# Three pairs of an output projection in Strassen's form, with their stage reordered

## The chip, the cores and the metric

The kernel runs on one core of one Trainium2 chip. TensorE (PE) multiplies, VectorE (DVE), ScalarE (ACT) and GpSimd (POOL) do the elementwise work, and SyncE (SP) issues nearly all the DMAs. Each engine takes its own instructions strictly in order and waits for the others through semaphores. The metric is the device time of one execution in microseconds, as the median of several runs.

## The reference

The kernel computes a transformer layer for 2048 tokens of 1024 features: linear attention with 32 heads of 32 features, then a gated feed-forward network (FFN) with 3584 hidden features. All inputs and the output are bf16.

```python
h  = x + A(layernorm(x), wqkv, wo)
h2 = h + B(layernorm(h), W_gate, W_up, W_down)

# A: q, k, v = split(x @ wqkv); phi(t) = where(t > 0, t + 1, exp(t)) + 1e-6
kv  = einsum("bhsd,bhse->bhde", phi(k), v)
z   = einsum("bhsd->bhd", phi(k))
num = einsum("bhqd,bhde->bhqe", phi(q), kv)
den = einsum("bhqd,bhd->bhq", phi(q), z)[..., None] + 1e-6
A   = (num / den) @ wo

# B: (relu(x @ W_gate) * (x @ W_up)) @ W_down
```

The change concerns the last line of A, `(num / den) @ wo`, and the addition of x to it.

## The kernel before

**Planning.** The program is written as calls of `PL.add(engine, ...)` and its wrappers `mm` (a matmul), `ident_act` (a copy on ACT), `dma` and `dma_t` (a transfer, or one that transposes, issued by SP). The order of the calls is the order on each engine. A `_Buf` remembers who wrote and read a buffer, and from that the waits are derived; `.over` names the buffers that lived in the same place before. So the order of work is written out by hand, mainly by functions put into lists (`hooks`) that are called between the products of a group.

**Stages.** Tokens come in 16 tiles of 128. The projections to k, v and q are made in Strassen's form by `sgroup`: of a pair of blocks on either side, seven products instead of eight, on four PSUM banks a, f, b and c. ACT copies the bank of one product to the next bank (`fk1`, `fk2`), so that later products accumulate on it; sums of inputs are made ahead on DVE. The FFN is in that form too: `t_sums` makes sums of its first weights (tiles T), `s_sums` the four sums S1 to S4 of the normalised h, `x_inner` and `w_inner1` sums for a second level of the scheme, and `ffn_unit` computes two gate or up column blocks at a time.

**The stage between.** It starts when the last q group has ended and its left-over feature maps (`late_phi`, two pairs of instructions at L879 and L882, on DVE) remain. One loop runs `t` from 4 to 20, with a lag of `LAG = NOT = 4` steps between numerators and projection:

```python
for t in range(NE, NST + LAG + 1):
    if LAG <= t < NST + LAG:
        a4_mm(t - LAG)
    if t < NST:
        a2_num(t)
        a2_div(t)
    if LAG <= t < NST + LAG:
        a4_h(t - LAG)
        run(late_phi, 1)
    if LAG + 1 <= t < TPP + LAG + 1:
        a4_norm(t - LAG - 1)
```

- `a2_num` (L1253) makes the numerators and denominators of one tile on PE: 32 small matmuls into banks 0 to 3.
- `a2_div` (L1264) divides on DVE: `dtmp` (L1270), `rden` (L1273) and `o` (L1275); then SP transposes o into a slot of the ring oT (`T3d`, L591).
- `a4_mm` (L1286) multiplies oT of a tile with wo: 2 halves of 512 columns, 8 matmuls each, into banks 4 and 5 or 6 and 7 in turn.
- `a4_h` (L1295) adds x in one DVE instruction of 128x1024 (`h`, L1299), stores h, and for tiles 0 to 7 starts the layer norm's statistics: two passes on ACT (L835) and four tiny POOL instructions (L841 to L1315).
- `a4_norm` (L1321) normalises on ACT one step later; SP then transposes into hnT (`T5d`).
- `load_x2` fetches x for a tile; the first eight have places of their own, the others share three.

Some of the FFN's preparation is spread over the same loop: from t = 9 one of the eight POOL sums of `t_sums` (L1401) per step, at t = 15 to 18 the sums S (L1377), at t = 4, 5, 17 and 18 a weight load. Then the FFN begins: the products P1 of its first unit, which are copied on to banks 4 and 5 by ACT, then P5, P2, P5, P6 and `r15` (L1625), whose second part R5 reads what `x_inner` (L1444) and `w_inner1` (L1422) made on DVE.

Of the kernel before, what the change touches and what calls it, by code (L numbers as in the profile page):

```python
# [6 lines left out]
ALU = mybir.AluOpType  # L7
# [125 lines left out]
def bass_sequential_preLN__linear_attn_block__glu_gated_reglu__prompt_kernel(  # L133
# [71 lines left out]
    with es:  # L205
# [8 lines left out]
        NV = 6  # L214
        NXN = 4
        NO = 4
        NOT = 4
        NDT = 4
        NWG = 6
        NTR = 4  # L220
# [4 lines left out]
        NWR = 2  # L225
        NSTAT = 4
        NX2 = 3
        NHS = 3
        NPH = 4

# [42 lines left out]
            return pk[:, i, :] if i < NPK else x1[:, i - NPK, :]  # L273

        osb = RE[:, 0:NO * D].rearrange("p (a b) -> p a b", a=NO)
        oT = RE[:, NO * D:(NO + NOT) * D].rearrange("p (a g t) -> p a g t", a=NOT, g=NG)
        ftmp = RE[:, 0:(NO + NOT) * D].bitcast(f32).rearrange("p (a b) -> p a b", b=SBW)
        c22 = RE[:, 2 * D:3 * D].rearrange("p (a b) -> p a b", b=SBW)
        c12 = RE[:, 3 * D:4 * D].rearrange("p (a b) -> p a b", b=SBW)
        xs5 = RE[:, 4 * D:6 * D].bitcast(f16).rearrange("p (j k t) -> p j k t", j=4, k=2)  # L280
        g5 = RE[:, 6 * D:8 * D].bitcast(f16).rearrange("p (s j c) -> p s j c", s=2, j=4)
        hnE = RE[:, 4 * D:8 * D].rearrange("p (t a c) -> p t a c", t=STB, c=P)
        o0 = (NO + NOT) * D
        x2r = RE[:, o0:o0 + NX2 * D].rearrange("p (a b) -> p a b", a=NX2)
        x2e = RC[:].rearrange("p (a b) -> p a b", a=TPP)

        def x2_slot(st):
            return st if st < TPP else TPP + st % NX2

        def x2(st):  # L290
            return x2e[:, st, :] if st < TPP else x2r[:, st % NX2, :]

        hl = RE[:, o0:o0 + 2 * D].rearrange("p (a b) -> p a b", a=2)
        xl = RE[:, o0 + 2 * D:o0 + 4 * D].rearrange("p (a b) -> p a b", a=2)
# [33 lines left out]
        D1 = RXH[:].bitcast(f16).rearrange("p (q t) -> p q t", t=SBW)  # L328
        Et = RX[:, 0:NPH * NW].rearrange("p (a b) -> p a b", a=NPH)
        btmp = RX[:, NPH * NW:(NPH + 4) * NW].bitcast(f32).rearrange("p (a b) -> p a b", a=2)  # L330

        def TWq(j):
            if j < 2:
# [27 lines left out]
        def bank(b, w=512):  # L361
            return ps[:, b, 0:w]
# [7 lines left out]
        def slots(name, n):  # L370
            return [_Slot(sem("%s%d" % (name, i))) for i in range(n)]
# [3 lines left out]
        sl_wkv = [slots("dwkv%d_" % i, 2) for i in range(NKV)]  # L375
        sl_wq = slots("dwq_", ND2)
        sl_wo = slots("dwo_", ND2)
        sl_x2 = slots("dx2_", TPP + NX2)
        sl_w = slots("dw_", NWG)
        sl_wd = slots("dwd_", NWS + NWX)  # L380
        sl_hr = slots("dhr_", NHR)
# [18 lines left out]
        def bufs(name, n):  # L400
            return [_Buf("%s%d" % (name, i)) for i in range(n)]
# [22 lines left out]
        B_dt = bufs("dt_", NDT)  # L424
        B_rd = bufs("rd_", NDT)
        B_oT = bufs("oT_", NOT)
        B_x2 = bufs("x2_", TPP + NX2)
        B_hs = bufs("hs_", NHS)
        B_hscr = bufs("hscr_", NST)
        B_hl = bufs("hl_", 2)  # L430
# [54 lines left out]
        def flat(x):  # L485
            return [b for row in x for b in (flat(row) if isinstance(row, list) else [row])]
# [5 lines left out]
            for b_ in B_pk[NPK + i]:  # L492
                b_.over = B_x1[i]
        kv_ring = flat(B_x1) + flat(B_pk) + flat(B_v) + [B_vones]
        for b_ in B_o + B_oT + B_x2[TPP:]:
            b_.over = kv_ring
        for b_ in B_x2[0:TPP]:
            b_.over = B_TWk
        for b_ in B_f + B_c22 + B_c12:
            b_.over = B_o + B_oT  # L500
        for b_ in B_hl + B_xl:
            b_.over = B_x2[TPP:]
        for b_ in flat(B_T):
            b_.over = B_wq
        for b_ in B_S:
# [15 lines left out]
            b_.over = flat(B_Sx[0:3])  # L521
        for b_ in B_hnT:
            b_.over = B_Sx[3] + B_TWq[0:2]
        for b_ in B_D1:
            b_.over = B_xn + B_hs
        for b_ in flat(B_lsum):
            b_.over = B_E + B_bt + [B_TWq[2]]
        for b_ in B_hres + B_ds:
            b_.over = B_lsum
        for b_ in B_outst:  # L530
            b_.over = B_E + B_bt + [B_TWq[2]]
        B_m5r.over = flat(B_wsum)
        for b_ in flat(B_g1a) + [B_m5a]:
            b_.over = flat(B_xnT) + flat(B_pqT)
        for b_ in B_xs1a:
            b_.over = B_E + B_bt + [B_TWq[2]]
        for b_ in B_hnE:
            b_.over = B_o + B_oT
        for b_ in B_V:
            b_.over = B_hnE  # L540
        for b_ in flat(B_hh) + B_out2:
            b_.over = flat(B_xnT) + flat(B_pqT)
        for b_ in flat(B_pqT):
            b_.over = flat(B_wkv)
        B_TWq[3].over = [B_zeros]
# [44 lines left out]
        def dma_t(slot, dst_ap, src_ap, name, reads=(), writes=()):  # L590
            return PL.add("sp", lambda e: e.dma_start_transpose(dst_ap, src_ap), reads=reads, writes=writes,  # L591
                          slot=slot, name=name)
# [301 lines left out]
        def run(ops, n):  # L894
            for _ in range(min(n, len(ops))):
                ops.pop(0)()
# [367 lines left out]
        def a2_div(st):  # L1264
            k = st % NO
            kd = st % NDT
            kt = st % NOT
            rb = [B_bank[b_] for b_ in NB]
            nv = ps[:, 0:HPG, 0:NG * NUW].rearrange("p h (g w) -> p g h w", w=NUW)
            PL.add("dve", lambda e: e.tensor_scalar(  # L1270
                out=dtmp[:, kd, :].rearrange("p (g h) -> p g h", h=HPG), in0=nv[:, :, :, Dh],
                scalar1=1e-6, scalar2=None, op0=ALU.add), reads=rb, writes=[B_dt[kd]], name="dtmp_%d" % st)
            PL.add("dve", lambda e: e.reciprocal(out=rden[:, kd, :], in_=dtmp[:, kd, :]),  # L1273
                   reads=[B_dt[kd]], writes=[B_rd[kd]], name="rden_%d" % st)
            PL.add("dve", lambda e: e.tensor_tensor(  # L1275
                out=osb[:, k, :].rearrange("p (g h e) -> p g h e", h=HPG, e=Dh),
                in0=nv[:, :, :, 0:Dh],
                in1=rden[:, kd, :].rearrange("p (g h) -> p g h", h=HPG).unsqueeze(3).to_broadcast([P, NG, HPG, Dh]),
                op=ALU.mult), reads=rb + [B_rd[kd]], writes=[B_o[k]], name="o_%d" % st)
            dma_t(sl_to[kt], oT[:, kt, :, :], osb[:, k, :], "T3d_%d" % st, reads=[B_o[k]], writes=[B_oT[kt]])  # L1280

        H_PAIRS = [4, 6]

        a4_bank = {}

        def a4_mm(st):  # L1286
            k = st % NOT
            b = a4_bank[st] = min(H_PAIRS, key=lambda b: max(bank_last[b], bank_last[b + 1]))
            for nt in range(ND2):
                touch_bank(b + nt)  # L1290
                for ct in range(NG):
                    mm(bank(b + nt, NW), oT[:, k, ct, :], wo[:, ct, nt * NW:(nt + 1) * NW],
                       ct == 0, ct == NG - 1, [B_oT[k], B_wo[nt]], B_bank[b + nt], "a4_%d_%d" % (st, nt))

        def a4_h(st):  # L1295
            xs = x2_slot(st)
            hs = st % NHS
            b = a4_bank.pop(st)
            PL.add("dve", lambda e: e.tensor_tensor(out=hsb[:, hs, :], in0=ps[:, b:b + 2, :],  # L1299
                                                    in1=x2(st).rearrange("p (a c) -> p a c", a=2), op=ALU.add),  # L1300
                   reads=[B_bank[b], B_bank[b + 1], B_x2[xs]], writes=[B_hs[hs]], name="h_%d" % st)
            if TPP <= st and st + NX2 < NST:
                load_x2(st + NX2)
            dma(sl_hs[hs], ov[st * P:(st + 1) * P, :], hsb[:, hs, :], "st_h_%d" % st, reads=[B_hs[hs]],
                writes=[B_hscr[st]])
            if st >= TPP:
                return
            ks = st % 2
            a4_k[st] = ks
            src = hsb[:, hs, :]  # L1310
            for f_ in act_stats(src, [B_hs[hs]], xn[:, st % NXN, :], B_xn[st % NXN], s2[:, ks, 0:4], B_s2[ks],
                                "ln2_%d" % st):
                f_()
            m_, r_, n_ = s2[:, ks, 0:1], s2[:, ks, 2:3], s2[:, ks, 4:5]
            PL.add("pool", lambda e: e.tensor_scalar(out=n_, in0=m_, scalar1=r_, scalar2=-1.0, op0=ALU.mult,  # L1315
                                                     op1=ALU.mult),
                   reads=[B_s2[ks][0], B_s2[ks][2]], writes=[B_s2[ks][4]], name="lnn_%d" % st)
# [3 lines left out]
        def a4_norm(st):  # L1321
            hs = st % NHS
            ks = a4_k[st]
            kx = st % NXN
            PL.add("act", lambda e: e.activation(out=xn[:, kx, :], in_=hsb[:, hs, :], func=ACTF.Identity,
                                                 bias=s2[:, ks, 4:5], scale=s2[:, ks, 2:3]),
                   reads=[B_hs[hs], B_s2[ks][2], B_s2[ks][4]], writes=[B_xn[kx]], name="norm2_%d" % st)
            dma_t(sl_tx[kx], hnT[:, :, st * P:(st + 1) * P], xn[:, kx, :], "T5d_%d" % st, reads=[B_xn[kx]],
                  writes=[B_hnT[st]])

# [908 lines left out]
                    for i in range(TPP + NX2):  # L2239
                        load_x2(i)  # L2240
        flush()
        LAG = NOT
        pool_t = t_sums(0, "pool")
        for t in range(NE, NST + LAG + 1):
            if LAG <= t < NST + LAG:
                a4_mm(t - LAG)
            if t < NST:
                a2_num(t)
                a2_div(t)
            if LAG <= t < NST + LAG:  # L2250
                a4_h(t - LAG)
                run(late_phi, 1)
            if LAG + 1 <= t < TPP + LAG + 1:
                a4_norm(t - LAG - 1)
            if t in (4, 5, 17, 18):
                load_w_next()
            if t >= 9:
                run(pool_t, 1)
            if 15 <= t < 19:
                s_sums()[t - 15]()  # L2260
        for q in range(NWR):
            load_wraw(q)
        load_w_next()
# [179 lines left out]
```

## Time and profile before

| What | Value |
|---|---|
| Runs | 717.06, 717.28, 717.21 us; median 717.21 |
| Profiled execution | span 714.8 us from its first to its last instruction; its device time is not listed apart |
| Granted TensorE clock | 1.000 over the span |
| The stage, 165.82 to 226.08 us | 60.26 us; PE busy 60.26, DVE 48.12, ACT 29.19, POOL 19.50 |
| Its last part, 204.45 to 226.08 us | 21.63 us; DVE busy 16.80, ACT 0.67, POOL 6.00 |

Lines of the timeline give the start in microseconds from the span's start, the duration in microseconds, the engine, the line of the kernel, the operation, out<-in by name, the shape, and how many equal instructions were merged (x16). In square brackets stands the idle time of the engine before, and what ended it. Names such as RE, RX, RXH, RC, RAB and RWG are large areas of SBUF in which several buffers live; ps is PSUM. A line of the chain gives start, duration, and what the time went to. A line of the windows gives the stretch, its length, the busy time and number of instructions of PE, PEld (weight loads), DVE, ACT and POOL, the granted clock, the busy share of the DMA engines and their GB/s.

### The profile page before, as it was taken

Reading aid. Unit: us, or ns where it says so; the run is one execution under the profiler, and the core shown is the slowest. Engines: PE = TensorE matmul, PEld = TensorE weight load, DVE = VectorE, ACT = ScalarE, POOL = GpSimd, SP = SyncE. Lnnn points to the kernel's source line nnn. Section 1 sums busy time; section 2 is a strip of 40 time slices with the busy share of each in tenths; the row PEclk is TensorE's granted clock in tenths of the full one; section 3 lists DMA queues with packets and bytes.
Section 4 is the critical chain, followed back from the end, with each engine's and each line's share of the span. In section 5 each row is a group of like instructions: output and inputs, shape, how many; then the busy total and the mean of one; then the engine's idle time right before and its main releaser. Section 6 shows DMA issues by size and latency. Waiting matters only on the chain.

```text
span 714.8 us, 13206 instructions
## 1 busy us (share of the span) xinstructions
PE 709.6 (99%) x5051; PEld 394.6 (55%) x5051; DVE 603.0 (84%) x964; ACT 404.3 (57%) x729; POOL 109.5 (15%) x178
## 2 busy tenths in 40 slices
PE   9999999999999999999999999999999999999998
PEld 4444444444444445455544558865555555548887
DVE  6988867899777799999998787878889888988984
ACT  4987667764841677777776411037666767633010
POOL 3221100000360223132312001310000000000331
PEclk9999999999999999999999999999999999999999
DMA  9853344015999799999897999995344544268996
GB/s 296 263 103 76 42 136 164 1 31 98 229 185 296 224 326 276 313 290 293 265 302 209 296 253 319 320 214 161 96 135 113 145 121 122 75 206 262 321 313 181
DMA packets 195103, 144.20 MB, mean 202 GB/s; under 512 B 53984, under 2 KB 172512, under 8 KB 195040
## 3 DMA queue, kind: packets, MB, share of 16 engines
q1 hardware_dynamic: 190048, 138.77, 66.9%
q0 software_dynamic: 4032, 3.67, 3.6%
q10 hardware_dynamic: 960, 0.92, 0.4%
q8 instruction: 40, 0.66, 0.4%
q14 instruction: 23, 0.19, 0.1%
HBM read 98.76 MB, written 32.51 MB: 184 GB/s over the span
## 4 chain that ended last, share of the span: by engine, by line
PE 95%; DVE 3%; DMA 1%; issue 1%; ACT 1%
PE ps L795 94%; DMA RAB<-RXH 1%; DVE RC L1018 0%; DVE RW L1018 0%; DVE RWG L1043 0%; DMA RE<-in_A_x_dram 0%; ACT RXH L835 0%; PE ps L956 0%; DVE RE L1796 0%; DVE st L809 0%; DVE RX L1134 0%; PE ps L935 0%; DVE RWG L1736 0%; DVE RH L1043 0%; DVE RE L1195 0%
## 5 line engine op out<-in xcount | busy, mean ns | idle before, releaser
L800 ACT ACTIVATE ps<-ps 128x512 f32<-128x512 f32 (+1 forms) x257 | 129.6, 516 | 188.7 <-PE ps L795 145.3
L795 PE MATMUL ps<-RC,RO 128*128 128x512 f16 x616 | 147.0, 369 | 0.0
L795 PEld LDWEIGHTS ps<-RC,RO 128*128 128x128 f16 x616 | 60.1, 98 | 53.2 <-ACT ps L800 1.2
L800 ACT ACTIVATE RE<-ps 128x512 f32<-128x512 f32 (+3 forms) x106 | 63.8, 627 | 32.2 <-PE ps L795 18.1
L795 PE MATMUL ps<-RC,RWG 128*128 128x512 f16 x320 | 80.9, 379 | 0.0
L795 PE MATMUL ps<-RH,RWG 128*128 128x512 bf16 (+1 forms) x348 | 77.7, 348 | 0.0
L795 PE MATMUL ps<-RH,RO 128*128 128x512 bf16 (+1 forms) x256 | 65.3, 379 | 0.0
L1805 POOL DMA_DIRECT2D out_dram<-RX x20 | 17.9, 1259 | 271.4 <-DVE RX L1796 218.3
L1535 DVE TENSOR_TENSOR RE<-ps,RE 128x1024 bf16<-128x1024 f32 (+1 forms) x42 | 44.0, 1047 | 18.2 <-PE ps L795 18.1
L795 PE MATMUL ps<-RW,RE 128*128 128x512 bf16 x256 | 57.6, 380 | 0.0
L795 PEld LDWEIGHTS ps<-RH,RWG 128*128 128x128 bf16 x348 | 34.0, 98 | 35.2 <-ACT ps L800 0.2
L795 PE MATMUL ps<-RW,RAB 128*128 128x256 f16 (+3 forms) x362 | 52.9, 301 | 0.0
L795 PE MATMUL ps<-RAB 128*128 128x512 bf16 (+2 forms) x238 | 49.8, 348 | 0.0
L795 PEld LDWEIGHTS ps<-RC,RWG 128*128 128x128 bf16 (+1 forms) x320 | 30.0, 98 | 34.4 <-ACT ps L800 5.8
L795 PEld LDWEIGHTS ps<-RW,RAB 128*128 128x128 f16 (+1 forms) x362 | 35.3, 98 | 14.5
L1535 DVE TENSOR_TENSOR RAB<-ps,RE 128x1024 bf16<-128x1024 f32 x28 | 34.2, 1221 | 10.1 <-PE ps L795 9.7
L1796 DVE TENSOR_TENSOR RE<-ps,RE 128x512 f32<-128x512 f32 x44 | 30.2, 686 | 14.4 <-PE ps L795 11.8
L1547 ACT ACTIVATE RAB<-RAB 128x1024 bf16<-128x1024 bf16 x28 | 29.5, 1053 | 19.6 <-DVE RAB L1535 19.6
L1535 DVE TENSOR_TENSOR RAB<-RAB,RE 128x1024 bf16<-128x1024 bf16 x56 | 37.2, 685 | 2.9 <-ACT RE L800 2.5
L795 PEld LDWEIGHTS ps<-RW,RE 128*128 128x128 bf16 x256 | 24.0, 98 | 27.9 <-DVE RXH L1299 0.4
L1401 DVE TENSOR_TENSOR RO<-RWG 128x1024 f16<-128x1024 bf16 x54 | 39.4, 729 | 0.0
L1401 DVE TENSOR_TENSOR RO<-RWG,RO 128x1024 f16<-128x1024 bf16 x54 | 38.2, 708 | 0.0
(188 smaller groups left out, 1229.1 us busy)
## 6 DMA issues: line engine op xcount, KB each, us to landing
RWG<-in_B_W_gate_dram SPq DMA_DIRECT2D x28, 512.0 KB, 5.9
RWG<-in_B_W_up_dram SPq DMA_DIRECT2D x28, 512.0 KB, 5.0
RW<-l_scr SPq DMA_DIRECT2D x20, 448.0 KB, 5.2
RW<-in_B_W_down_dram SPq DMA_DIRECT2D x14, 512.0 KB, 6.3
t_scr<-RW SPq DMA_DIRECT2D x14, 512.0 KB, 4.5
l_scr<-RX SPq DMA_DIRECT2D x7, 1024.0 KB, 9.5
RE<-l_scr SPq DMA_DIRECT2D x15, 448.0 KB, 4.5
RE<-in_A_x_dram SPq DMA_DIRECT2D x23, 256.0 KB, 3.7
```

Of the source, the lines that this page charges most:

```text
L795: lambda e: e.matmul(out_ap, lhsT, rhs, start=start, stop=stop, skip_group_check=skip),
L800: PL.add("act", lambda e: e.activation(out=dst, in_=src, func=func), reads=reads, writes=writes, name=name)
L1401: PL.add(eng, lambda e: e.tensor_tensor(out=tb(j, u), in0=f0(u), in1=f1(u), op=ALU.subtract), reads=[B_w[i + x] for x in r] + ([B_T[k + x] ...
L1535: PL.add("dve", lambda e: e.tensor_tensor(out=dst, in0=in0, in1=in1, op=op), reads=reads, writes=writes, name=name)
L1547: PL.add("act", lambda e: e.activation(out=d, in_=d, func=ACTF.Relu), reads=[], writes=db, name=name)
L1796: PL.add(eng, lambda e: e.tensor_tensor(out=dst, in0=in0, in1=in1, op=op), reads=reads, writes=writes, name=name)
L1805: PL.add("pool", lambda e: e.dma_start(dst, src, accum_op=ALU.add), reads=[bsrc], writes=[B_hscr[st]], slot=sl, name="acc_%d_%d" % (st, dh))
```

## The change

Tiles 0 to 9 (`NDIR = 10`) are projected as before. Tiles 10 and 11, 12 and 13, 14 and 15 become three groups in Strassen's form (`o_group`), with seven products of four matmuls each.

- The sums of wo (`wo_sums`, tiles TWo) are made on POOL, in eight instructions of half a matrix each: two before the loop, six after the steps 0 to 5.
- The sums of oT (`o_sums`, So1 to So4 per pair) are made on DVE, but for one of the first pair on POOL.
- In the groups, POOL adds x to the two shared parts (`add_x`, named ox). In the first two groups (`act_first`), the two direct outputs go through an ACT copy and a POOL add, and in the last one they are read by DVE. The other two are finished by DVE from a bank and the shared part.
- Numerators move to places within the projections (`at`); they run ahead of their use by other distances, and oT gets six slots (two of them in the area RX). Transposes of the normalised tiles 4 to 7 are issued later (`a4_t`). x of the tiles 12 to 15 gets places of its own in the area RA, loaded during the groups. The POOL sums of `t_sums`, the sums S and two weight loads move later.

```diff
-        NOT = 4
+        NOT = 6
+        NDIR = 10
 
+            dma_t(sl_to[kt], oT(st), osb[:, k, :], "T3d_%d" % st, reads=[B_o[k]], writes=[B_oT[kt]])
...
+        def wo_sums(j, eng, k0, k1):
...
+            x, y = {2: lambda: (w(1, 1), w(0, 1)), 0: lambda: (w(0, 1), w(0, 0)), 1: lambda: (w(1, 1), t(0)),
+                    3: lambda: (w(1, 0), t(1))}[j]()
+            PL.add(eng, lambda e: e.tensor_tensor(out=t(j)[0], in0=x[0], in1=y[0], op=ALU.subtract),
+                   reads=x[1] + y[1], writes=[B_TWo[j]], name="TWo%d" % (j + 1))
...
+        def o_group(p, bks, hooks, act_first):
+            sa, sb2 = 2 * p, 2 * p + 1
+            a, f, b, c = bks
+            s7, sc = (btmp[:, 1, :], B_bt[1]), (btmp[:, 0, :], B_bt[0])
...
+            def add_x(src, st, h, dst=None):
+                x, bx = res(st, h)
+                d, db = src if dst is None else dst
+                PL.add("pool", lambda e: e.tensor_tensor(out=d, in0=src[0], in1=x, op=ALU.add),
+                       reads=[bx] + ([] if dst is None else [src[1]]), writes=[db], name="ox_%d_%d" % (st, h))
+
+            def fin(st, h, bk, s=None):
+                d, db = half(st, h)
+                if s is not None:
+                    PL.add("dve", lambda e: e.tensor_tensor(out=d, in0=bank(bk), in1=s[0], op=ALU.add),
+                           reads=[B_bank[bk], s[1]], writes=[db], name="h_%d_%d" % (st, h))
+                elif act_first:
+                    ident_act(Ef[:, h, :], bank(bk), [B_bank[bk]], [B_Ef[h]], "oc_%d_%d" % (st, h))
+                    add_x((Ef[:, h, :], B_Ef[h]), st, h, (d, db))
+                else:
+                    x, bx = res(st, h)
+                    PL.add("dve", lambda e: e.tensor_tensor(out=d, in0=bank(bk), in1=x, op=ALU.add),
+                           reads=[B_bank[bk], bx], writes=[db], name="h_%d_%d" % (st, h))
...
+            prod(a, X(0, 0), W(0, 0), True, "P1")
+            ident_act(bank(b), bank(a), [B_bank[a]], [B_bank[b]], "ofk1")
+            hook(1)
+            prod(f, SX(2), TW(2), True, "P7")
+            ident_act(s7[0], bank(f), [B_bank[f]], [s7[1]], "os7")
+            add_x(s7, sb2, 0)
+            hook(2)
+            prod(b, SX(1), TW(1), False, "P6")
+            ident_act(bank(c), bank(b), [B_bank[b]], [B_bank[c]], "ofk2")
+            hook(3)
+            prod(a, X(1, 0), W(1, 0), False, "P2")
+            fin(sa, 0, a)
+            hook(4)
+            prod(c, SX(0), TW(0), False, "P5")
+            ident_act(sc[0], bank(c), [B_bank[c]], [sc[1]], "osc")
+            add_x(sc, sb2, 1)
+            hook(5)
+            prod(b, X(1, 1), TW(3), False, "P4")
+            fin(sb2, 0, b, s7)
+            hook(6)
+            fin(sb2, 1, f, sc)
+            store(sb2)
+            prod(c, SX(3), W(1, 1), False, "P3")
+            o_pend[1] = [lambda: fin(sa, 1, c), lambda: store(sa)]
+            hook(7)
...
-        LAG = NOT
         pool_t = t_sums(0, "pool")
...
+        at = {0: {15: [nd]}, 1: {14: [nd]}, 2: {13: [nd]}, 3: {11: [nd]}, 4: {9: [nd]}, 5: {7: [nd]},
+              6: {5: [nd]}, 7: {3: [nd]}, 8: {2: [nd, t5(4)]}, 9: {2: [nd, t5(5)]}}
+        aft = {0: [tw(2, 0)], 1: [tw(2, 2)], 2: [tw(1, 0)], 3: [tw(1, 2)], 4: [tw(3, 0)], 5: [tw(3, 2)],
+               8: sums(p0, (2, "pool")), 9: sums(p0, (0, "dve"), (1, "dve"), (3, "dve"))}
+        tw(0, 0)()
+        tw(0, 2)()
+        for d in range(NDIR):
+            a4_mm(d, at.get(d, {}))
+            a4_h(d)
+            run(late_phi, 1)
+            if 1 <= d <= TPP:
+                a4_norm(d - 1)
+            if d < 2:
+                load_w_next()
+            for f_ in aft.get(d, ()):
+                f_()
+            if d in (6, 7, 8):
+                run(pool_t, 1)
+        o_group(p0, [4, 6, 5, 7], {
+            2: [nd], 4: sums(p0 + 1, (2, "dve"), (0, "dve")), 5: [nd, lambda: load_x2(13), lambda: load_x2(12)],
+            6: sums(p0 + 1, (1, "dve"), (3, "dve")) + [t5(6), t5(7)]}, True)
+        load_w_next()
+        o_group(p0 + 1, [4, 2, 5, 7], {
+            1: [lambda: run(pool_t, 1)], 2: sums(p0 + 2, (2, "dve"), (0, "dve"), (1, "dve"), (3, "dve")),
+            3: [lambda: run(pool_t, 1), lambda: load_x2(15), lambda: load_x2(14)], 6: [ss[0], ss[1]]}, True)
+        load_w_next()
+        run(pool_t, 1)
+        o_group(p0 + 2, [4, 6, 5, 7], {2: [ss[2]], 4: [ss[3]]}, False)
+        for f_ in o_pend.pop(1):
+            f_()
+        run(pool_t, len(pool_t))
```

`nd` is `a2_num` and `a2_div` of the next tile. `tw(j, k0)` is half a weight sum, `t5` a held-back transpose, `ss` the four sums S, and `p0` is 5, the first pair in the new form. In `at`, the number before a list is the matmul (0 to 15) of that tile before which its entries are placed.

## The prediction

> **What bounds the kernel now.** I read the page first (busy shares, slices), then the chain that ended last, then the windows of the stage that the change rewrites, and last its timeline, engine by engine.
>
> ```profile
> PE 709.6 (99%) x5051; PEld 394.6 (55%) x5051; DVE 603.0 (84%) x964; ACT 404.3 (57%) x729; POOL 109.5 (15%) x178
> 44.03 630.50 PE ps L795 x4452
> 165.82:226.08 60.26, 60.26 (x641) 27.25 (x640) 48.12 (x66) 29.19 (x43) 19.50 (x40) 1.00 0.92 208
> 188.69 0.37 PE L795 MATMUL ps<-kvz,RAB 32*128 32x33 bf16 x32
> 189.00 3.63 PE L795 MATMUL ps<-RW,RE 128*128 128x512 bf16 x16
> 192.56 0.37 PE L795 MATMUL ps<-kvz,RAB 32*128 32x33 bf16 x32
> ```
>
> The first line is the page's: TensorE busy for 99% of the span. The second is the chain's: from 44.03 us it is 630.5 us of matmuls and nothing else. The third is the stage's window (total, then PE, PEld, DVE, ACT, POOL, granted clock, DMA share, GB/s): TensorE covers all 60.26 us at clock 1.00, and VectorE is at 80% (48.12). The last three are one step: numerators at 188.69, 16 matmuls from 189.00, the next numerators at 192.56, so 3.87 us. Single matmuls of 512 columns start 0.2159 us apart in the trace; 16 are 3.45 us and the numerators take the other 0.41. Check: 256 x 0.2159 + 12 x 0.41 = 60.2 us, the window. There is no slack on TensorE: a matmul less is a gain, and a wait is a loss.
>
> **What is removed.** A pair of tiles takes 2 x 2 x 8 = 32 matmuls, in Strassen's form 7 x 4 = 28. Three pairs: 12 x 0.2159 = 2.59 us off the path. The twelve numerators remain. The forks (ACT copying one bank to the next between products) are those of the projection stages, whose matmuls after a fork start 0.238 and 0.249 us after the one before instead of 0.216; two a group make 6 x 0.03, call it +0.2 us. So with full cover: -2.4 us.
>
> **What is added, and where it lies.** Weight sums: 8 POOL instructions of 128x1024. The nearest rows are 128x512 (1.152 us) and 128x256 (0.668), so 0.184 + 1024 x 0.00189 = 2.12 us each. The first two run before the loop, the others one a step behind the statistics of layer norm. Per pair: four sums of 128x512 (DVE 0.42 us as in L1043, POOL 1.15) and four adds of x or, in the first two groups, two on the shared halves and two behind an ACT copy; so 4, 4 and 2 POOL adds of 128x512 f32 (1.15 us, from L1796's undisturbed ones). In exchange the six h of 1.21 us on DVE become 8 of 0.69. Five of the eight POOL sums of the first FFN weights (1.15 us, before at 196 to 210 us) and all of S1 to S4 (1.21 us each, DVE, before among plain tiles) now fall among or behind the groups. Count of POOL work from the second group on: 7 adds and 5 sums, 13.8 us, where the trace had 6.0 us in the last 21.6. Whether that is hidden depends on whether POOL and DVE can run at once:
>
> ```profile
> 257.76 1.22 POOL L774 TENSOR_TENSOR RAB<-RW 128x256 f16<-128x256 bf16 x1 [2.19 <-PE ps L795]
> 258.37 1.16 DVE L1401 TENSOR_TENSOR RO<-RWG,RO 128x1024 f16<-128x1024 bf16 x1
> 259.45 0.68 DVE L1401 TENSOR_TENSOR RO<-RWG 128x1024 f16<-128x1024 bf16 x1
> 673.00 3.04 POOL L1796 TENSOR_TENSOR RE<-RE,RX 128x512 f32<-128x512 f32 x2 [1.13 <-DVE RE L1796]
> 675.17 1.83 DVE L1736 TENSOR_TENSOR RWG<-RAB 128x1792 f16<-128x1792 bf16 x1
> 205.40 1.23 DVE L1275 TENSOR_TENSOR RE<-ps,rden 128x1024 bf16<-128x1024 f32 x1
> 205.96 2.26 POOL L1401 TENSOR_TENSOR RO<-RWG 128x512 f16<-128x512 bf16 x2
> ```
>
> At 257.76 a POOL instruction of 0.67 us takes 1.22 because a DVE sum with both inputs in SBUF is under way; the next DVE sum then takes 1.16 instead of 0.68: each waits for the other's whole instruction, in order of arrival. The same at 673 to 677 for just the POOL add that the groups use (two in 3.04; a DVE sum of 1.08 takes 1.83). DVE work that reads PSUM (205.40) runs at its usual 1.23 beside POOL. So sums on DVE (So, S, x_inner, g1) and everything on POOL must be laid end to end; evacuations need not. That decides two places.
>
> **Place one: numerators of tile 7.**
>
> ```profile
> 175.63 1.21 DVE L1299 TENSOR_TENSOR RXH<-ps,RC 128x1024 bf16<-128x1024 f32 x1
> 176.47 0.27 POOL L1315 TENSOR_SCALAR s<-s 128x1 f32<-128x1 f32 x1
> 176.76 0.28 DVE L879 TENSOR_SCALAR RX<-RX 128x512 bf16<-128x512 bf16 x1
> 177.08 0.69 DVE L882 SCALAR_TENSOR_TENSOR RAB<-RXH,RX 128x512 bf16<-128x512 f32 x1
> 178.52 1.23 DVE L1275 TENSOR_TENSOR RE<-ps,rden 128x1024 bf16<-128x1024 f32 x1
> ```
>
> After h of tile 1 DVE still has a late feature map (176.76, 177.08; both inputs in SBUF), then o of tile 6 (178.52 to 179.75). At 176.47 POOL ends the statistics of tile 0, and there, some 0.22 us later, the change queues a 2.12 us weight sum: 176.7 to 178.8. The feature map then waits, and dtmp, rden and o of tile 6 queue behind it: o ends 2.0 to 2.1 us later, near 181.8. Before, numerators 7 came at 180.97; now they stand before matmul 11 of tile 3, at 177.40 + 11 x 0.2159 = 179.78, and need o's banks. TensorE waits 2.0 us. Bounds: 0 (the two DVE forms are not seen blocked in the trace; only tensor-tensor sums are) and 2.1; I take 2.0 since L882 too reads twice from SBUF. [...] Later steps have only PSUM readers on DVE, and per step 1.33 us of statistics and 2.12 of sums fit POOL's 3.87.
>
> **Place two: from the second group into the FFN.** Time 0 is the start of the first group; a product is 0.863 us, numerators 14 and 15 lie inside, so the groups would begin at 0, 6.87, 12.9 and the FFN at 19.0. Numerators 15 start at 4.73; dtmp, rden and o end at 7.2; their transpose lands about 3.7 us later (the stage's 14 transposes: 3.5 median, 5.2 worst), at 10.9. SP issues x of tiles 13 and 12 only behind that transpose and its 1.24 us of issuing: they land at 12.2 and 12.7 (3.7 median). DVE stops at the four sums of the third pair until the transpose lands, and everything behind it waits: h of tile 13, S1, S2, h, S3, and on to the FFN. POOL, free at 9.25, has its adds and weight sums queued. Laid end to end in order of arrival: add 10.4, T 11.6, So3 12.0, (x of 13) So1 12.4, add 13.5, So2 14.0, T 15.1, So4 15.5, add 16.7 beside h of tile 13 (16.2), S1 17.9, add 19.1, S2 20.3, T 21.4, S3 22.6, add 23.8, S4 25.0, add 26.1, add 27.3, h of tiles 15 and 14 until 28.7, behind two more T (29.6), x_inner 31.2, g1 31.6. TensorE needs h of tile 13 by 14.2 (fork of the third group into that bank: first loss, 2.1 us) and x_inner and g1 at R5 of the first FFN unit, 19.0 + 6.05 + 0.2 = 25.2. It gets there at 31.6: +6.3 us in all, the first 2.1 within it. The bounds: without the mutual blocking the same queue gives h of 13 at 14.1, the last h at 22.8 and g1 at 24.9, just before 25.2, so 0; a transpose landing at 12.3 adds 1.3 to 6.3. I take 6.3, because the rows at 673 to 677 are the same two kinds of instruction. [...]
>
> At no cost: the six-deep oT ring, x slots in the dead xnT region, hp homes (their buffers' last readers are steps back). Transposes 4 to 7 of h are held back on SP; needed by S1, issued by 10.8, covered. The up weights move behind the store of tile 13 on SP (21.4, landing near 27), hidden only while DVE is later than that.
>
> **Sum.** -2.59 + 0.2 + 2.0 + 6.3 = +5.9 us. The profiled execution's span is 714.8 us; the median of the runs is 717.21, 2.4 more, which lies outside the span and stays. 714.8 + 5.9 + 2.4 = 723.1 us.
>
> **Rivals.** (a) *POOL and DVE overlap after all* (this is the other side: one mechanism, decided by whether g1 is ready before 25.2 us after the first group's start). Against it stand 258.37 and 675.17; for it, that without blocking every deadline is just met. Time: 717.2 - 2.4 = 714.8. (b) *Only place one bites*: POOL's queue in the groups finds gaps. 717.2 - 2.4 + 2.0 = 716.8, no change. (c) *Only place two bites*, L879 and L882 being immune: 717.2 - 2.4 + 6.3 = 721.1. Fewer matmuls than said is excluded: the groups' loops give 28.
>
> **How the numbers follow.** Forecast (both places) 0.55, (c) 0.2, (a) 0.16, (b) 0.09. Two rows of the same kinds of instruction carry the blocking; what I am less sure of is the order in some twenty-five steps of a ledger. A measurement of this kernel tells some 0.2% (1.4 us) from no change: 715.8 to 718.6. Faster 0.16, same 0.08, slower 0.76. Range: from (b)'s 716.8 to 725.5 (6.3 with a late transpose, +1.3, and about 1 us of ACT waits behind blocked evacuations). Where cases of both signs count, the forecast's own range is 721 to 725.5.
>
> **What would show it.** In the changed profile: 244 large matmuls in the stage; a gap on TensorE of about 2 us in tile 3 with L879 or L882 of some 2 us; DVE sums of 128x512 at 0.9 to 1.6 us instead of 0.42, S at above 2; a gap in the third group and one of about 4 us before R5 of the first FFN unit. Wrong if the chain stays unbroken TensorE there (then (a)), or if the sums keep 0.42 and 1.21 us with POOL busy beside them.

## The result, and the profile after

The changed kernel takes 722.36 us (median of 4 runs, 721.81 to 723.06) against 717.25 for the kernel before beside it (median of 4): ratio 1.0067 [1.0049, 1.0085], slower by 5.1 us. The forecast was 723.1. The profiled execution has a span of 720.4 us and a time of 722.16; before, the span was 714.8, so the two profiled executions differ by 5.6 us. One execution of one of the experiments' kernels (the last under "The loads of x earlier") took 2335.95 us; its median there is of its other three. The first row below is the page's busy shares, the second the window that the prediction shows for the kernel before (same columns), and the others are the longest waits of TensorE in this stage (who waits, for whom, us in total, times, longest; some 0.3 of the 2.1 us lie elsewhere):

```profile
PE 703.7 (98%) x4984; PEld 392.3 (54%) x5039; DVE 615.3 (85%) x978; ACT 413.0 (57%) x745; POOL 143.0 (20%) x197
165.82:226.08 60.26, 54.81 (x606) 24.41 (x616) 53.26 (x75) 36.62 (x57) 42.70 (x53) 1.00 0.87 182
PE ps L831 <- DVE RE L1311: 3.3, 2, 1.8
PE ps L831 <- ACT ps L836: 2.1, 4, 1.0
PE ps L831 <- ACT RX L836: 0.8, 1, 0.8
PE ps L831 <- DVE RAB L1602: 0.8, 1, 0.8
```

GpSimd does 33.5 us more, 23.2 of them in this window (42.70 against 19.50), and VectorE does 5.1 more in the window. TensorE was busy for all of the 60.26 us before and is for 54.81 now, at the same full clock (1.00): it does not work slower, it waits. The chain that ended last was matmuls without a break before; between the first group and the FFN it now runs through other engines, among others (start, us, what):

```profile
206.48 5.71 DMA RE<-RE
212.21 2.66 DVE RAB L1363 x2
218.59 3.31 DMA RAB<-in_A_x_dram
229.06 2.13 POOL RXH L1406
231.19 3.22 POOL RX L1406 x2
```

The measure used below, called the stage, is the time from the first numerators of the stage to R5 of the first FFN unit: 164.64 to 232.35 before (67.71 us), 165.25 to 238.42 after (73.17): +5.46. The rest of the spans differs by 0.6 us ahead of the stage and by -0.5 behind it. TensorE's gaps in that stretch, beyond the usual spacing, are 1.91 us before numerators 7; 0.28 in the first group; 1.65 and 0.34 in the second; 1.12 and 0.79 in the third (the trace shows 1.01 there, but the record of one matmul of 0.22 us is missing); 0.91 and 0.93 in the first FFN unit. They come to 7.93; with 2.59 us of matmuls saved that is 5.34, against 5.46 measured.

**Place one** in the timeline of GpSimd, VectorE and TensorE (start, us, engine, line, operation, out<-in):

```profile
177.51 2.12 POOL L1346 TENSOR_TENSOR RAB<-RW 128x1024 f16<-128x1024 bf16 x1
177.57 2.21 DVE L915 TENSOR_SCALAR RX<-RX 128x512 bf16<-128x512 bf16 x1
179.81 0.71 DVE L918 SCALAR_TENSOR_TENSOR RAB<-RXH,RX 128x512 bf16<-128x512 f32 x1
181.12 1.23 DVE L1311 TENSOR_TENSOR RE<-ps,rden 128x1024 bf16<-128x1024 f32 x1
182.40 0.37 PE L831 MATMUL ps<-kvz,RAB 32*128 32x33 bf16 x32 [1.84 <-DVE RE L1311]
```

L915 and L918 are the late feature map (L879 and L882 before). The weight sum starts 0.06 us ahead of it, and the 0.28 us instruction takes 2.21. It is the tensor_scalar that is blocked, for GpSimd's whole instruction, and L918 then runs at its usual 0.7. The numerators of tile 7 (last row) wait for o, the row before.

**Place two**, VectorE and GpSimd together, from the landing of the transpose of tile 13 on:

```profile
212.14 1.15 POOL L1406 TENSOR_TENSOR RXH<-RX,RE 128x512 bf16<-128x512 f32 x1 [1.40 <-ACT RX L836]
212.21 2.66 DVE L1363 TENSOR_TENSOR RAB<-RE 128x512 f16<-128x512 bf16 x2 [0.76 <-DMA RE<-RE]
213.25 1.34 POOL L1406 TENSOR_TENSOR RX<-RX,RE 128x512 f32<-128x512 f32 x1
215.39 1.23 DVE L1311 TENSOR_TENSOR RE<-ps,rden 128x1024 bf16<-128x1024 f32 x1
216.67 1.04 PE L831 MATMUL ps<-RAB 128*128 128x512 f16 x4 [1.49 <-DVE RE L1311]
224.86 2.13 POOL L1406 TENSOR_TENSOR RX<-RX,RAB 128x512 f32<-128x512 f32 x1
226.01 2.06 DVE L1544 TENSOR_TENSOR RC<-RC,RH 128x2048 f16<-128x2048 f16 x1
226.96 2.13 POOL L1568 TENSOR_TENSOR RO<-RWG 128x512 f16<-128x512 bf16 x1
229.06 2.13 POOL L1406 TENSOR_TENSOR RXH<-RX,RAB 128x512 bf16<-128x512 f32 x1
```

Two sums (L1363) of 0.42 us take 2.66 beside two adds of x (L1406); o of tile 15 (L1311) stands behind them, and TensorE waits for its banks. Later an add of 1.15 us takes 2.13 and a sum S of 1.21 takes 2.06 (the other three S take 1.57). The pattern is that of the rows at 257 and 673 us in the prediction: in these rows each waits until the other's instruction has ended.

### The profile page after: what moved, and what is told of

It reads as the page before. It is cut to its first block, busy times and chain, and to the rows that moved or that the text cites. A ratio compares the mean times of both kernels' runs of the same rounds, so it can differ in the third digit from the quotient of the medians.

```text
span 720.4 us, 13204 instructions
## 1 busy us (share of the span) xinstructions
PE 703.7 (98%) x4984; PEld 392.3 (54%) x5039; DVE 615.3 (85%) x978; ACT 413.0 (57%) x745; POOL 143.0 (20%) x197
## 4 chain that ended last, share of the span: by engine, by line
PE 81%; DVE 11%; issue 3%; DMA 2%; POOL 2%; ACT 1%; SPq 0%; DVEq 0%; POOLq 0%
PE ps L831 81%; DVE RE L1311 1%; DVE RX L915 1%; DVE RAB L918 1%; DVE RO L1568 1%; DMA RE<-RE 1%; POOL RX L1406 1%; DVE RW L767 1%; DMA RAB<-RXH 1%; DVE RXH L1460 1%; DVE RC L1054 0%; DVE RAB L1702 0%; POOL RXH L1406 0%; DMA RAB<-in_A_x_dram 0%; DVE rden L1309 0%
## 5 line engine op out<-in xcount | busy, mean ns | idle before, releaser
L836 ACT ACTIVATE ps<-ps 128x512 f32<-128x512 f32 (+1 forms) x263 | 133.0, 517 | 181.2 <-PE ps L831 127.9
L1972 POOL DMA_DIRECT2D out_dram<-RX x20 | 17.9, 1232 | 271.2 <-DVE RX L1963 218.4
L831 PE MATMUL ps<-RAB 128*128 128x512 bf16 (+3 forms) x272 | 58.8, 352 | 3.0 <-DVE RE L1311 1.5
L831 PE MATMUL ps<-RH,RO 128*128 128x512 bf16 (+1 forms) x228 | 59.2, 379 | 1.5
L831 PE MATMUL ps<-RW,RAB 128*128 128x256 f16 (+3 forms) x368 | 55.2, 302 | 1.1 <-ACT RX L836 0.8
L836 ACT ACTIVATE RX<-ps 128x512 f32<-128x512 f32 (+1 forms) x47 | 27.5, 597 | 25.6 <-PE ps L831 20.5
L831 PEld LDWEIGHTS ps<-RAB 128*128 128x128 bf16 (+1 forms) x274 | 26.0, 98 | 28.3 <-ACT ps L836 3.2
L831 PEld LDWEIGHTS ps<-RH,RO 128*128 128x128 f16 (+1 forms) x256 | 24.4, 98 | 24.6 <-ACT RX L836 1.5
```

The lines of the kernel that those rows point to most:

```text
L831: lambda e: e.matmul(out_ap, lhsT, rhs, start=start, stop=stop, skip_group_check=skip),
L836: PL.add("act", lambda e: e.activation(out=dst, in_=src, func=func), reads=reads, writes=writes, name=name)
L1972: PL.add("pool", lambda e: e.dma_start(dst, src, accum_op=ALU.add), reads=[bsrc], writes=[B_hscr[st]], slot=sl, name="acc_%d_%d" % (st, dh))
```

## The experiments

Two theories. **Shared resource**: the loss is that sums on VectorE with both inputs in SBUF and elementwise work on GpSimd exclude each other. **Late inputs**: sums or not, the groups come at a pace at which o, its transpose, and x arrive late, whatever GpSimd does. The stage is as above, from one profile each (67.71 before, 73.17 after); times and ratios are medians against the kernel before on the same chip. Runs of one kernel differ by up to 3.7 us, so a difference of under 1 us between two stages is weak evidence.

**Place one alone.** The second weight sum, first half, goes ahead of the loop:

```
-        aft = {0: [tw(2, 0)], 1: [tw(2, 2)], ...
+        aft = {1: [tw(2, 2)], ...
         tw(0, 0)()
         tw(0, 2)()
+        tw(2, 0)()
```

> Only edit against the changed kernel: the half weight sum that stood behind the statistics of tile 0 goes before the loop, as a third one there. Blocking theory (a DVE feature map with its inputs in SBUF waits out the 2.12 us POOL sum, and o of tile 6 and numerators 7 behind it): the gap of 2.0 us on TensorE before numerators 7 goes, L915 there falls from 2.21 to 0.28 us; 722.4 - 2.0 to 2.2 = 720.3 us. Rival (the numerators stand too early for a DVE that is full): the gap stays, 722.4 us.

Measured: 720.98 us (719.68 to 722.52), ratio 1.0055 [1.0037, 1.0074], 0.7 us slower than forecast; stage 72.29, so -0.88. In VectorE's timeline of this kernel the feature map is back to its own duration:

```profile
177.28 0.28 DVE L915 TENSOR_SCALAR RX<-RX 128x512 bf16<-128x512 bf16 x1
177.60 0.69 DVE L918 SCALAR_TENSOR_TENSOR RAB<-RXH,RX 128x512 bf16<-128x512 f32 x1
```

The wait before numerators 7 is gone, so its cause is shown. But of the 1.91 us only 0.88 reach R5 in these two profiles, and 1.4 in the medians: 0.62 us come back as a wait for a transpose of o (at 189.94), the wait before the second group's first product with a sum grows from 1.65 to 1.99, and the third group loses 2.3 in place of 1.9. What stands behind is not set by TensorE's pace alone.

**Place two: GpSimd without reading.** In the groups, each add of x and each of the last five GpSimd weight sums becomes two memsets of the same tile (0.55 us each, so that the engine stays about as long busy); the kernel leaves out these x and these sums. The edit of the adds (that of the weight sums is alike):

```
-                PL.add("pool", lambda e: e.tensor_tensor(out=d, in0=src[0], in1=x, op=ALU.add),
+                for _ in range(2):
+                    PL.add("pool", lambda e: e.memset(d, 1.0),
```

> The changed kernel with its POOL adds of x in the groups, and the last five POOL sums of the first FFN weights, each replaced by two memsets of the same destination: same places in the queue, same waits, about the same POOL time (0.53 us a memset of 128x512 bf16), but nothing is read from SBUF. The x of these parts and these weight sums are left out. Blocking theory (POOL's reads and the second SBUF input of a DVE sum exclude each other): DVE sums fall to 0.42 and 1.21 us, POOL's instructions keep their own length, most of the loss behind the first group (6.3 us) goes: 716.5 to 718.5 us. Rival (POOL's queue is simply too long, or transposes and loads of x come too late): the same queue, 721.5 to 722.5 us.

Measured: 718.37 us, ratio 1.0020 [1.0010, 1.0031], within the blocking theory's forecast and 3 us below the rival's; stage 69.25, so -3.92. VectorE and GpSimd of this kernel, at the same two points:

```profile
211.84 1.11 POOL L1407 MEMSET RXH<- 128x512 bf16 x2 [1.46 <-ACT RX L836]
211.89 0.76 DVE L1363 TENSOR_TENSOR RAB<-RE 128x512 f16<-128x512 bf16 x2 [0.72 <-DMA RE<-RE]
213.19 1.23 DVE L1311 TENSOR_TENSOR RE<-ps,rden 128x1024 bf16<-128x1024 f32 x1
223.01 1.11 POOL L1571 MEMSET RO<- 128x512 f16 x2
223.10 1.23 DVE L1545 TENSOR_TENSOR RC<-RC,RH 128x2048 f16<-128x2048 f16 x1
```

GpSimd is under way at each sum, and the pair takes 0.76 instead of 2.66, S 1.23 instead of 2.06. The memsets keep 1.11 a pair. So in these rows it is not GpSimd being busy that costs, but its reading at the same time. Of the 6.0 us lost in place two, 3.9 go away. Left are the wait of place one and some 2.2 us of small waits, it seems behind the last two x above all: VectorE waits 2.23 us for one of them to land. So late inputs probably have a share too, the smaller one.

**Fewer weight sums among the groups.** On top of the moved sum, two weight sums a step run on GpSimd from step 6 on and none in the groups; then also with VectorE adding x directly (`act_first` False):

```
-            if d in (6, 7, 8):
-                run(pool_t, 1)
+            if d >= 6:
+                run(pool_t, 2)
```

> As e1_sum_moved, and the eight POOL sums of the first FFN weights run two a step behind the projections of tiles 6 to 9, where DVE reads PSUM; none is left in the groups. Blocking theory: five times 1.15 us leave the shared queue of POOL and DVE sums, g1 comes some 5 us sooner: 720.3 - 4 = 716.3 us (715.5 to 717.5). Rival (the late transpose of tile 15 and the loads of x behind it start the loss): 719.5 to 720.5 us.

> As e3_T_early, and in the first two groups the two direct outputs are read by DVE from PSUM with x (0.69 us each) instead of an ACT copy and a POOL add (1.15 us): four POOL adds less in the shared queue, 2.8 us more on DVE, which do not exclude POOL. Blocking theory: another 0.5 to 1 us, 715.5 us (714.8 to 716.3). Rival (DVE's own load is the bound now): slower than e3_T_early by 1 to 2 us.

Measured: 720.84 us, 1.0055 [1.0037, 1.0073], and 721.58, 1.0056 [1.0041, 1.0071]; stages 72.31 and 72.59. Both gains failed to come; the rivals were nearer. The stage of the first is what it was (72.29) with the weight sums in the groups. The sums had only changed places: So3 of the first pair, on GpSimd, comes behind them and costs 1.18 us before the first product with a sum, and the last two x land only near 230 us and cost 1.52 and 1.86. With the adds on VectorE, TensorE waited 1.91 us for o of tile 15; some 1.7 us of this second kernel's time is clock and not queue, as the last section shows.

**The loads of x earlier.** With x of tiles 12 to 15 loaded behind steps 2 to 5 (`load_x2(10 + d)`), then with the weight sums on VectorE too (`t_sums(0)`), then with o of tile 15 ahead of the sums of the second pair, and last with the second group adding x on VectorE. The edit that swaps the order, from the second kernel to the third:

```
-            2: [nd], 4: sums(p0 + 1, (2, "dve"), (0, "dve")), 5: [nd],
-            6: sums(p0 + 1, (1, "dve"), (3, "dve")) + ...
+            2: [nd], 5: [nd] + sums(p0 + 1, (2, "dve")),
+            6: sums(p0 + 1, (0, "dve"), (1, "dve"), (3, "dve")) + ...
```

> As e1_sum_moved, with x of the tiles 12 to 15 loaded behind the steps 2 to 5 instead of behind transposes and weights within the groups. Queue theory (POOL's own instructions and the DVE sums, laid end to end, set when g1 is ready; the loads are hidden behind them): no change to e1_sum_moved within 0.7 us, 720 to 721 us. Rival (late x is a cause by itself): 718 to 719 us.

> As e5_x_early, and the sums of the first FFN weights on DVE in four instructions of 128x2x512 (0.7 us each), three behind the tiles 6 to 8, one at the end; POOL makes none. 5.75 us leave the shared queue, 0.7 enter it, and no x is late: with both causes gone, 717.5 us (716.5 to 718.5), about level with the kernel before. Rival (neither matters once numerators 15 and the transpose behind them are late): 720 us.

> As e6_T_on_DVE, and of the four input sums of the second pair none stands before o of tile 15 on DVE: o no longer waits for the transpose of tile 13 and for POOL's adds. o of tile 15 ends about 2.5 us sooner (7.1 instead of 9.6 us after the first group's start); the sums themselves come some 0.5 us late for the second group. 716.3 us (715.3 to 717.3). If the late o is not a cause: as e6_T_on_DVE.

> As e7_o_first, with the two direct outputs of the second group read by DVE from PSUM instead of an ACT copy and a POOL add: 2.3 us leave the shared queue, DVE gets 1.4 more. 715.8 us if the shared queue still bounds, 716.5 to 717 if DVE does.

Measured, in that order: 724.3 us, 1.0098 [1.0083, 1.0113]; 720.3, 1.0040 [1.0025, 1.0055]; 718.02, 1.0014 [1.0004, 1.0024]; 720.43, 1.0044 [1.0027, 1.0061]. Stages: 75.11, 71.73, 69.68, 71.38. The first went against both theories, by over 3 us. The second came out at its rival's 720, though taking the weight sums off GpSimd gained 4.0 us over the first; the third missed its forecast by 1.7 but gained 2.3; the fourth went against both of its figures, by over 3 us. One transpose in SP's queue, first in the kernel with place one alone, then in the first kernel here, with one of the early loads ahead of it, and VectorE and TensorE in that kernel:

```profile
206.39 1.45 SPq L627 DMA_TRANSPOSE RE<-RE  x1
187.70 1.40 SPq L623 DMA_DIRECT2D RAB<-in_A_x_dram  x1
209.24 2.96 SPq L627 DMA_TRANSPOSE RE<-RE  x1
214.97 2.33 DVE L1363 TENSOR_TENSOR RAB<-RE 128x512 f16<-128x512 bf16 x2 [3.01 <-DMA RE<-RE]
219.10 3.38 PE L831 MATMUL ps<-RAB 128*128 128x512 f16 x8 [3.41 <-DVE RE L1311]
```

The transpose of o of tile 13 is issued at 206.39 in the first of these kernels and at 209.24 in the second, whose first group starts only 0.6 us later; it lands 5.7 us after its issue in both. Ahead of it SP has spent 3.0 us on issuing the four loads. VectorE stands idle for 3.01 us at the sums that need the transpose, and o of tile 15, which needs only matmuls long done, stands behind them. So the loads were not free: they delay the transposes that SP issues behind them, and the order on VectorE turns that delay into TensorE's. Swapping the order alone (second kernel to third) is worth 2.05 us in the stage, though some 1.5 of what the second loses is its clock, as the last section shows. VectorE's direct adds in the fourth gave a wait of 1.24 us for one of them (L1419) and 1.29 for a fork behind it; it seems that VectorE had no room for them.

**The queue and the order, apart.** The loads go ahead of the loop and two held-back transposes are issued at once, so that SP's queue is short in the groups; once with o first, once with the sums first.

```
+        for st in range(NXR, NST):
+            load_x2(st)
         tw(0, 0)()
```

> As e7_o_first, but x of the tiles 12 to 15 is loaded before the loop instead of behind the steps 2 to 5, and the transposes of the normalised tiles 4 and 5 are issued at once, not held back to tiles 8 and 9. SP theory (in e7 the oT transposes of tiles 9 to 13 came late because SP issues them in turn with these loads, 1.3 us a transpose): the transpose of tile 13 lands by 4 us after the first group's start instead of 8, the waits of P7 for So3 of the first and second pair (1.24 and 1.0 us) go: 715.7 us (715.0 to 716.5), faster than the kernel before. Rival (the transposes are late by DMA bandwidth, not by SP's order): as e7_o_first, 718.

> As e10_queue_o_first, with two sums of the second pair before o of tile 15 again, as the change has them. If the transpose of tile 13 lands in time, they fit into DVE's idle 1.2 us before o of tile 15, and P6 of the second group does not wait for So2: 715.2 us (714.6 to 716.2). If it lands late, o waits behind them: 718 us.

Measured: 717.7 us, 1.0007 [0.9997, 1.0017]; and 719.99, 1.0037 [1.0025, 1.0050]. Stages 68.07 and 70.58. The order is worth 2.3 us in the medians, again. The second missed both of its figures (715.2 and 718). The forecast for the first was 2 us too low, and its time is that of its rival, by which the transposes are late by DMA bandwidth and not by SP's order. The transpose of tile 13 was issued 1.75 us after the group's start (3.12 in the third kernel above), but landed 6.8 us after it (8.9 there), not 4: it took 5.0 us from issue to landing, against the median of 3.5 in the prediction. Why it is so slow was not tested. And 2.7 us of waits remain (0.86 for So3 of the first pair, which GpSimd forms, 0.61 for the second pair's sums, 0.80 for h of tile 13, 0.43 for a transpose).

**The order alone, in the changed kernel, and two of the last waits.**

> The changed kernel with one edit: VectorE forms o of tile 15 before the sums of the second pair instead of behind two of them. In the changed kernel o of tile 15 ended 9.64 us after the first group's start and TensorE lost 1.65 us there. If that order is a cause of its own, o ends some 2 us sooner, its transpose too, and the whole queue behind it starts sooner: 722.4 - 1.7 = 720.7. Rival: what sets the end is the amount of GpSimd and VectorE sums laid end to end, which is the same, so that R5 of the first FFN unit is reached no sooner and the wait only moves to later gaps: 722 to 722.5.

> From e10, two sums are placed differently: the first sum of the first pair (So3_5) goes from GpSimd to VectorE, between the two halves of h of tile 9, and the last sum of the third pair (So4_7) goes behind the first shared half of h of tile 13. In e10 the first product with a sum waited 0.86 us for the former, and the third group's fork 0.80 us for h of tile 13, which stood behind four sums slowed by GpSimd's adds. If those two waits end where the queue says, 0.4 of the 0.86 and all of the 0.80 go: 717.7 - 1.2 = 716.5, level with the kernel before or a hair under. Rival: the time saved comes back at the next wait (the second product of the second group, or the fork before the first FFN unit), as it did when the first stall was taken away in e1: 717.3 to 717.7.

Measured: the changed kernel with only o first 721.13 us, 1.0054 [1.0042, 1.0067], stage 71.70, so -1.47, near the forecast. The medians of the two kernels differ by 1.2, and their runs at a mean clock of 1.000 do not overlap: 720.26 to 721.14 us in four with o first, 721.81 to 722.55 in three without. So the order is a cause of its own. The other (So3 of the first pair on VectorE between the halves of h of tile 9; So4 of the third pair behind h of tile 13) 716.85, 0.9998 [0.9989, 1.0007], stage 66.94; its forecast was 716.5, the rival's 717.3 to 717.7. In the first, VectorE reads:

```profile
213.18 1.22 DVE L1311 TENSOR_TENSOR RE<-ps,rden 128x1024 bf16<-128x1024 f32 x1
214.32 0.41 DVE L1363 TENSOR_TENSOR RAB<-RE 128x512 f16<-128x512 bf16 x1
```

o of tile 15 starts 2.2 us sooner than in the changed kernel, and the sums, now after GpSimd's two adds, keep 0.41. In the second, both waits named are gone, and a wait of 0.68 for the third group's last product remains beside the 0.61. Its stage is 0.77 us shorter than that of the kernel before, but its time cannot be told from it: in the profile its stage begins 1.5 us later (166.18 against 164.64). In the changed kernel, too, 0.6 us are lost ahead of the stage, where a DMA near 43 us lands 0.8 late. Whether this lateness is there in every run of these kernels stays open.

## Why the prediction was right

*Matmuls saved.* Each product of a group has its 4 matmuls of 0.2159 us in the timeline. Nothing shows the 0.2 us set aside for forks as a term of its own; the sum of the gaps leaves 0.1 for them.

*Place one.* Forecast 2.0, measured 1.91 in the changed kernel, by an instruction named (L879 before, L915 now). But the prediction took 2.0 because L882 reads twice from SBUF, and L882 (L918 now, 0.71 us) was not held up; the tensor_scalar ahead of it was (2.21 us for 0.28), a form that no row of before showed blocked. The moved sum took the wait away.

*Place two.* Forecast 6.3, measured 6.0 (the seven gaps from the first group on). g1 ends 31.4 us after the first group's start; the ledger had 31.6. The mechanism is the one forecast: without GpSimd's reads the sums are back at 0.42 and 1.23, and 3.9 us go. Some 2.2 us stay, though, where the ledger without blocking had none, probably for inputs that come later than it has them.

*What was mis-sized within it.* The ledger put o of tile 15 at 7.2 us after the group's start and the first loss in the third group (2.1). In fact o ended at 9.64, because the order of VectorE's queue was followed too loosely: So3 and So1 of the second pair stand ahead of it, they waited for the transpose of tile 13 to land, and then took 2.66 beside two adds. So the first loss came one group sooner (1.65 and 0.34), and the third group's fork lost 1.12. The gap of about 4 us before R5, named as a sign, is not there: 0.93 us are lost there, and the rest is spread over six gaps before it. The lag then shrinks down the queue. In us after the group's start, measured against the ledger: h of tile 13 17.5 (16.2), S1 19.0 (17.9), S2 21.1 (20.3), S3 23.2 (22.6), S4 25.3 (25.0), the last h 28.7 (28.7). The term that was too large is the turn: a GpSimd instruction and a sum S laid end to end were put at 1.15 + 1.21 = 2.36, but GpSimd's rows at 224.86, 226.96 and 229.06 are 2.10 apart, so some 0.25 us of each turn does overlap. That the two errors cancel is luck; the total is better than its parts.

*Rivals.* (a) no blocking: ruled out by the rows at 177 and 212 us. (b) and (c): both places lose. (c) said that L915 would be immune; it is not (2.21 us for 0.28).

*The sum.* 714.8 + 5.9 = 720.7 for the span, measured 720.4. The 2.4 us outside the span were too large: they set the span of one execution against the median of others. Where time and span of the same execution are listed they differ by 1.7 to 2.0 us, 1.8 in the changed kernel's profiled one (722.16 - 720.4). The 0.6 there and the 0.3 in the span make 723.1 into 722.16; the median is 0.2 above it. Between the medians the change costs 5.1 us, 0.8 less than the 5.9 of the sum.

*What the prediction did not see* is that about a quarter of place two is order, not amount: with o first in the changed kernel 1.5 of 6.0 us go although GpSimd's and VectorE's work is the same.

## What to carry to other kernels

Before sums are given to GpSimd to relieve VectorE, list what VectorE does beside them with both inputs in SBUF, or as a tensor_scalar on SBUF: in this case these and GpSimd's reads ran nearly end to end (2.10 us a turn of a GpSimd instruction and a sum S, where 2.36 is no overlap at all; 2.21 for a tensor_scalar of 0.28 beside a weight sum), so among them a sum moved to GpSimd still cost VectorE its time. In a queue written out by hand, what frees PSUM banks goes ahead of what waits for a DMA: that swap was worth 1.2 to 2.3 us in three pairs of kernels, in one of them 1.5 of it by the clock, against 2.6 saved in matmuls. A stall taken away is counted at the next deadline (here R5 of the first FFN unit), not where it stood: 1.91 us removed gave 0.88 in the stage and 1.4 in the medians.

## What was not expected of the hardware

TensorE's clock fell after some of its longer waits. In the profiles of three of the experiments a wait of 1.9, 2.65 or 3.6 us in the second group was followed, at once or 1.4 us later, by seven or eight matmuls that each took twice as long (granted clock 0.50 in all three). The windows of the kernel with the loads behind steps 2 to 5 (columns as in the prediction, the granted clock before the DMA share):

```profile
216.00:218.00 2.00, 0.00 (x0) 0.00 (x0) 1.93 (x5) 0.00 (x0) 1.01 (x1) 1.00 0.63 118
220.00:221.00 1.00, 1.00 (x4) 0.37 (x3) 1.00 (x2) 0.76 (x2) 0.17 (x1) 0.50 0.74 147
223.00:225.00 2.00, 2.00 (x11) 0.71 (x9) 1.97 (x3) 1.35 (x3) 2.00 (x3) 1.00 0.99 253
```

The granted clock is 0.50 from about 219 to 222 us and costs 1.5 us on top of the wait. In their profiles no such fall came after the changed kernel's waits of 1.91 and 1.65 us, nor after the 1.99 in the kernel with place one alone (granted clock 1.00 over the stage in both). It came after 2.65 and 3.6 us, but also, in the kernel with early weight sums and VectorE adding x, after a wait of 1.9 us with smaller ones around it; so these profiles show no length of a wait from which the clock falls. So part of what those kernels lost, 1.5 to 1.7 us each, is clock and not queue. The same program falls in some executions only: in the kernel of the memsets the mean clock is 0.998 in five of ten runs (718.77 to 720.96 us) and 0.999 or more in the others (717.27 to 717.97), so its median of 718.37 holds a part of this too, and without it GpSimd's reads are worth a little more.
